# Attention visits placed 64 products earlier in a fused attention and feed-forward kernel

## The chip, the cores and the metric

The kernel runs on one core of a Trainium2 chip, as one program. The metric is the device time of one execution in microseconds; where several executions were timed, their median. The profile is of one execution.

## The reference

One transformer block on 2048 rows of width 1024, in bfloat16: windowed causal attention with 32 heads of 32, then a dense layer pair with SiLU, each behind a layer norm without gains, each added to its input.

```python
qkv = layernorm(x) @ wqkv                      # q, k, v of 32 heads, 32 wide
scores = q @ k.T * 32 ** -0.5                  # kept where 0 <= query - key < 256
h = x + (softmax(scores) @ v) @ wo
h2 = h + silu(layernorm(h) @ w1) @ w2          # w1: 1024 x 3584, w2: 3584 x 1024
```

## The kernel before

**Stages.** The 2048 rows are four blocks (0 to 3) of 512. The order of all work is written out by hand. After a start-up that normalises block 0 and makes its values (v), there are these stages, each made of groups of eight matmuls of 128x128 by 512 columns that accumulate in one PSUM bank. Such a matmul is called a *product* here.

1. Query and key groups of block 0: 16 groups, 128 products (`qk_group`, L262, copied out in L264 by ScalarE and VectorE in turn).
2. Block 1: 8 groups of v (`v_group`, L252 and L254) and 16 of queries and keys, 192 products.
3. Blocks 2 and 3, the same: 384 products.
4. The output projection of blocks 0 to 2 (`wo_group`, L283): 24 groups, 192 products. Its residual add on VectorE (L285) empties the bank, and each finished tile of 128 rows is stored to `h_dram` (L288) and later loaded again (L642) for the second layer norm.
5. The dense layers, block by block: 28 groups against w1 (`h1_group`, L746, with tanh in L755 and the product in L756), then w2 (L783, L798). The projection of block 3 lies among the w1 groups of block 0.

**Attention lies between the products.** The 32 heads are eight groups of four (G = 8) in each block; a group of heads is numbered i = 8 b + g. Before every product the function `between` of a stream object counts it and may issue one of two things:

- a *visit*: the score matmuls of some heads, the exps on ScalarE that read them, and the masks on GpSimd (`select`, L411). Block 0 has one visit per half of a head group (`scores_0`, matmuls L392, exps L401 to L403). Blocks 1 to 3 have three visits for a pair of head groups (`visit`, matmuls L360, exps L315, L321 and L322).
- a *piece*: the matmuls of two heads' probabilities with v (`attn_piece`, L421), into one PSUM bank `o_ps`, which VectorE then divides by the row sums (`attn_norm`, L432 and L433). Every second piece puts a DMA transpose (L441, on SP) on the list `late`, which is run ahead of the next group. It writes the result over the queries.

**Where they stand.** `First` counts from block 1's start: a visit of block 0 every 12 products, and from the fourth visit on a piece just ahead of it. `Stream` counts from block 2's start: pair p has its visits at products 4, 20 and 36 of 48 p, and its four pieces at 42, 47, 58 and 63. So a pair has 48 products; 12 pairs fill stages 3 and 4, block 0's last three pieces are done at the head of stage 3, and the last two pieces of all are left over (`rest`, `pending`) and issued behind the first two w1 groups.

**Shared buffers.** Scores have one tile `sc` of four PSUM banks, written by every visit; its next writer waits for ScalarE to have read it. There are four more banks. Three take the groups' sums in turn, each emptied by VectorE after its group; the fourth is `o_ps`. A visit also borrows these: `idle` is the bank of the next group, `behind` that of the group before, `out` is `o_ps`. Exp results lie in buffers (`xbuf`, `ybuf`, `c_ring`) of two or three copies.

**Layer norm steps.** The layer norm of the next block is cut into steps on VectorE (four of statistics, L193 and L201; four of the reciprocal root, L209 to L216; four that normalise, L221) and four DMA transposes on SP (L225). One follows most groups, from n = 1. In the projection, the second layer norm's steps for block 0 begin after group 11, the load of h after group 9, two steps a group from 14.

VectorE, ScalarE, GpSimd and SP each take their instructions in the order written.

Of the kernel before, what the change touches and what calls it, by code (L numbers as in the profile page):

```python
# [14 lines left out]
P = 128  # L15
# [32 lines left out]
def kernel(  # L48
# [280 lines left out]
    def visit(i, n):  # L329
# [4 lines left out]
        if n == 0:  # L334
            own, e_own = unit_xy(i, 0), xbuf(i)
            more = [(0, idle, unit_c(i)), (1, out, unit_c(i)), (2, behind, unit_c(i))]
        elif n == 1:
            own, e_own = unit_xy(i, 1), ybuf(i)
            more = [(3, idle, unit_c(i)), (0, behind, unit_xy(i + 1, 0)), (1, out, unit_xy(i + 1, 0))]
        else:  # L340
            own, e_own = unit_xy(i + 1, 1), ybuf(i + 1)
            more = [(2, out, unit_xy(i + 1, 0)), (3, behind, unit_xy(i + 1, 0))]
# [34 lines left out]
    def scores_0(g, odd):  # L377
# [20 lines left out]
        for pair in range(2):  # L398
            e = (ybuf if odd else xbuf)(g)[:, 1024 * pair:1024 * (pair + 1)].rearrange("p (h q) -> p h q", q=512)
            two = sc[:, pair * 2:pair * 2 + 2, :]  # L400
            nc.scalar.activation(out=e[:, :, 0:256], in_=two[:, :, 0:256], func=ACT.Exp, scale=scale)  # L401
            nc.scalar.activation(out=e[:, :, 320:512], in_=two[:, :, 256:448], func=ACT.Exp, scale=scale)
            nc.scalar.activation(out=c_ring[:, (g + 1) % 3, pair * 2:pair * 2 + 2, 128 + 64 * odd:192 + 64 * odd],  # L403
                                 in_=two[:, :, 448:512], func=ACT.Exp, scale=scale)
            select(e[:, :, 0:P], e[:, :, 0:P], True)
            select(e[:, :, 256:384], e[:, :, 320:448], False)
            select(e[:, :, 384:512], e[:, :, 384:512], True)
# [42 lines left out]
    class First:  # L450


        def __init__(self):
            self.pieces, self.done, self.seen = [], 0, 0

        def between(self, kt):
            if self.seen == self.done * 12:
                if self.done > 2:
                    attn_piece(*self.pieces.pop(0))
                scores_0(self.done // 2, self.done % 2)  # L460
                self.pieces.append((self.done // 2, self.done % 2))
                self.done += 1
            self.seen += 1

    class Stream:


        def __init__(self, left):
            self.seen = 0
            self.visits, self.pieces = {}, {0: left[0], 10: left[1], 15: left[2]}  # L470
            for p in range((NB - 1) * G // 2):
                i, t = G + 2 * p, 48 * p + 4
                for n in range(3):
                    self.visits[t + 16 * n] = (i, n)
                for n in range(4):
                    self.pieces[t + (38, 43, 54, 59)[n]] = (i + n // 2, n % 2)

        def between(self, kt):
            if self.seen in self.pieces:
                attn_piece(*self.pieces.pop(self.seen))  # L480
            if self.seen in self.visits:
                visit(*self.visits.pop(self.seen))
            self.seen += 1

        def rest(self):
            assert not self.visits
            return [self.pieces[at] for at in sorted(self.pieces)]

# [180 lines left out]
    stream = First()  # L669
# [12 lines left out]
    stream = Stream(stream.pieces)  # L682
    for b in range(2, NB):
# [12 lines left out]
        for n in range(24):  # L696
# [32 lines left out]
    pending = [lambda piece=piece: attn_piece(*piece) for piece in stream.rest()]  # L729
# [106 lines left out]
```

## Time and profile before

| | |
|---|---|
| median of 3 runs | 698.19 us (696.15 to 698.81) |
| the profiled execution | 696.58 us, of which the span from first to last instruction is 694.9 us |
| instructions | 14583 |
| granted TensorE clock | 1.00 throughout |
| HBM | 39.85 MB read, 8.39 MB written |

By stage, in microseconds from the span's start (edges read from the timeline):

| stage | from, to |
|---|---|
| start-up | 0, 20.6 |
| queries and keys of block 0 | 20.6, 48.2 |
| block 1, with block 0's attention | 48.2, 102.7 |
| blocks 2 and 3, with attention of blocks 1 and 2 | 102.7, 225.5 |
| projection of blocks 0 to 2, with attention of block 3 | 225.5, 290.1 |
| dense layers | 290.1, 694.9 |

How to read the rows: PE is TensorE's matmul, PEld its weight load, DVE is VectorE, ACT ScalarE, POOL GpSimd, SP the queue that issues DMAs. A timeline row gives the start, the length, engine, line, operation, tile written and tiles read, shapes, the count of instructions that are merged in it, and in brackets the engine's idle time before it and what ended that. The matmul's length includes a modelled pipeline; starts are what to compare. A group row ends with busy time, mean ns of one, and idle time before it. A row of waits gives total, times and longest.

### The profile page before, as it was taken

The numbers are of one execution on the slowest core, as the hardware profiler recorded it, in microseconds if no ns is written. First come the engines' busy times: TensorE is split into PE (matmuls) and PEld (weight loads), VectorE is DVE, ScalarE is ACT, GpSimd is POOL, SyncE is SP. The second block draws the span as 40 slices with busy tenths as digits, with TensorE's granted clock in tenths as the row PEclk, the third lists the DMA queues.
The fourth block names the chain that finished last, engine by engine and source line by source line (L and its number), as shares of the span: only waits on it lengthen the run. The fifth ranks groups of instructions, "written<-read, shape, count | busy, mean of one in ns | idle before, by whom it ended". The sixth has DMA issues, their size and how long they took to land.

```text
span 694.9 us, 14583 instructions
## 1 busy us (share of the span) xinstructions
PE 676.7 (97%) x6084; PEld 340.4 (49%) x6200; DVE 290.2 (42%) x614; ACT 241.9 (35%) x462; POOL 160.8 (23%) x295
## 2 busy tenths in 40 slices
PE   9999999999999997999999999999999999999998
PEld 4445555555555554544444444444444444444445
DVE  5268646744444457443316134434133251233111
ACT  7326666656666664521310023300033200233000
POOL 1016765576666655500000000000000000000000
PEclk9999999999999999999999999999999999999999
DMA  8741241027321895791123410023300024100010
GB/s 275 254 92 40 48 108 32 17 48 210 116 75 34 283 227 176 169 337 62 31 77 99 106 39 1 0 76 83 84 1 0 12 97 91 46 1 0 31 38 24
DMA packets 77617, 61.50 MB, mean 89 GB/s; under 512 B 52464, under 2 KB 60656, under 8 KB 77552
## 3 DMA queue, kind: packets, MB, share of 16 engines
q1 hardware_dynamic: 77408, 60.31, 31.5%
q8 instruction: 48, 0.79, 0.5%
q10 hardware_dynamic: 144, 0.26, 0.1%
q14 instruction: 17, 0.14, 0.1%
HBM read 39.85 MB, written 8.39 MB: 69 GB/s over the span
## 4 chain that ended last, share of the span: by engine, by line
PE 89%; ACT 5%; issue 2%; DVE 2%; DMA 1%; POOL 0%; ACTq 0%; DVEq 0%
PE hacc L783 16%; PE hacc L746 16%; PE bank L262 13%; PE bank L746 12%; PE bank L783 12%; PE bank L252 5%; PE bank L421 5%; PE bank L283 4%; ACT r_e L321 4%; PE sc L360 2%; PE bank L360 2%; ACT r_e L322 1%; PE bank L566 1%; PE hacc L283 1%; PE sc L392 1%
## 5 line engine op out<-in xcount | busy, mean ns | idle before, releaser
L411 POOL TENSOR_SCALAR_AFFINE_SELECT r_e<-r_e 128x512 bf16<-128x512 bf16 (+1 forms) x288 | 157.8, 564 | 130.3 <-ACT r_e L321 61.6
L783 PEld LDWEIGHTS <-r_a 128*128 128x128 bf16 x952 | 90.8, 98 | 103.0
L746 PEld LDWEIGHTS <-r_w 128*128 128x128 bf16 x896 | 87.4, 98 | 105.2
L783 PE MATMUL hacc<-r_a 128*128 128x512 bf16 (+2 forms) x550 | 114.0, 366 | 0.5
L746 PE MATMUL hacc<-r_e,r_w 128*128 128x512 bf16 x375 | 84.7, 379 | 0.5
L783 PE MATMUL bank<-r_a 128*128 128x512 bf16 (+1 forms) x386 | 81.0, 368 | 0.4
L755 ACT ACTIVATE r_n<-hacc 128x512 f32<-128x512 f32 x24 | 14.3, 597 | 172.2 <-PE hacc L746 122.7
L262 PEld LDWEIGHTS <-r_w 128*128 128x128 bf16 x512 | 46.5, 97 | 52.0 <-issue 1.0
L264 DVE CAST r_a<-bank 128x512 bf16<-128x512 f32 x56 | 38.6, 689 | 61.8 <-PE bank L262 48.3
L746 PE MATMUL bank<-r_e,r_w 128*128 128x512 bf16 x282 | 63.6, 379 | 0.3
L262 PE MATMUL bank<-r_t,r_w 128*128 128x512 bf16 x233 | 56.4, 379 | 2.3 <-issue 1.6
L262 PE MATMUL bank<-r_w 128*128 128x512 bf16 x240 | 55.9, 379 | 1.4 <-issue 0.8
L421 PEld LDWEIGHTS <-r_e 128*128 128x128 bf16 x1440 | 45.6, 96 | 18.6 <-issue 3.9
L321 ACT ACTIVATE r_e<-sc 128x1536 bf16<-128x1536 f32 x36 | 53.5, 1485 | 0.0
L283 PE MATMUL bank<-r_o,r_a 128*128 128x512 bf16 x201 | 49.8, 379 | 2.0 <-issue 1.1
L421 PE MATMUL bank<-r_a,r_e 128*128 128x33 bf16 x1440 | 46.2, 178 | 2.9 <-DVE r_n L433 2.9
L315 ACT ACTIVATE r_e<-bank 128x512 bf16<-128x512 f32 x48 | 26.1, 598 | 55.9 <-PE bank L360 53.6
L798 DVE SCALAR_TENSOR_TENSOR r_t<-bank,r_t 128x512 bf16<-128x512 f32 (+1 forms) x14 | 9.3, 663 | 67.5 <-PE bank L783 67.5
L798 DVE SCALAR_TENSOR_TENSOR r_t<-hacc,r_t 128x512 bf16<-128x512 f32 (+2 forms) x20 | 13.0, 650 | 52.6 <-PE hacc L783 52.6
L283 PEld LDWEIGHTS <-r_a 128*128 128x128 bf16 x256 | 22.9, 97 | 24.6
L360 PEld LDWEIGHTS <-r_a 32*64 32x64 bf16 x1536 | 21.2, 103 | 17.9 <-issue 16.5
L252 PE MATMUL bank<-r_w,r_t 128*128 128x512 bf16 x116 | 28.3, 379 | 1.2 <-issue 0.8
(103 smaller groups left out, 586.4 us busy)
## 6 DMA issues: line engine op xcount, KB each, us to landing
r_w<-in_B_w_dram SPq DMA_DIRECT2D x8, 896.0 KB, 5.3
r_a<-in_B_w_dram SPq DMA_DIRECT2D x7, 1024.0 KB, 9.0
r_w<-in_A_wqkv_dram SPq DMA_DIRECT2D x4, 1024.0 KB, 8.4
h_dram<-r_t SPq DMA_DIRECT2D x16, 256.0 KB, 2.4
r_t<-h_dram SPq DMA_DIRECT2D x16, 256.0 KB, 3.0
out_dram<-r_t SPq DMA_DIRECT2D x31, 128.0 KB, 1.7
r_e<-h_dram SPq DMA_DIRECT2D x3, 1024.0 KB, 5.8
r_o<-in_A_x_dram SPq DMA_DIRECT2D x11, 256.0 KB, 4.3
```

Source lines behind the costliest of these rows:

```text
L252: nc.tensor.matmul(acc, lhsT=lnT_b[b % 2][:, kt, j * P:(j + 1) * P], rhs=wv[:, kt, c * 512:(c + 1) * 512], start=(kt == 0), stop=(kt == KT ...
L262: nc.tensor.matmul(acc, lhsT=wqk[:, kt, col0:col0 + P], rhs=lnT_b[b % 2][:, kt, :], start=(kt == 0), stop=(kt == KT - 1))
L264: copy(out=(qT, kT)[which][b][:, g, :], in_=acc)
L283: nc.tensor.matmul(acc, lhsT=qT[b][:, g, j * P:(j + 1) * P], rhs=wo[:, g, c * 512:(c + 1) * 512], start=(g == 0), stop=(g == G - 1))
L315: nc.scalar.activation(out=c_ring[:, lo:hi + 1:hi - lo, h, :], in_=four[bank].rearrange("p (n q) -> p n q", q=256), func=ACT.Exp, scale=scale)
L321: nc.scalar.activation(out=tri_of(e)[:, h0:h1, :, 64:256], in_=tri, func=ACT.Exp, scale=scale)
L360: nc.tensor.matmul(bank[half * 64:half * 64 + 64, col:col + qb - qa], lhsT=kT[t // 4][r0:r0 + DH, g, k0:k0 + 64], rhs=qT[b][r0:r0 + DH, g, ...
L411: nc.gpsimd.affine_select(out=dst, in_=src, pattern=[[0, n] for n in dst.shape[1:-1]] + [[sgn, P]], compare_op=ALU.is_ge if upper else ALU ...
L421: nc.tensor.matmul(o_ps[:, qt * 2 + hh, 0:VW], lhsT=chunk_of(i, bank, piece, pair * 2 + hh), rhs=v[:, b * 4 + kt, g * 4 + pair * 2 + hh, : ...
L746: nc.tensor.matmul(acc, lhsT=w1[:, kt, ft * P:(ft + 1) * P], rhs=ln2T[b][:, kt, :], start=(kt == 0), stop=(kt == KT - 1))
L783: nc.tensor.matmul(acc[:, 0:c1 - c0], lhsT=gT[:, ft, j * P:(j + 1) * P], rhs=w2[ft // 4][:, ft % 4, c0:c1], start=(ft == 0), stop=(ft == F ...
L798: nc.vector.scalar_tensor_tensor(out=t_out[j % 2][:, c0:c1], in0=acc[:, 0:c1 - c0], scalar=0.5, in1=t_in[j % 2][:, c0:c1], op0=ALU.mult, o ...
```

## The change

One class `Attention` takes the place of `First` and `Stream`. It counts from the first product of stage 1.

- Block 0's 16 visits stand every 10 products from product 92, so the first four fall in stage 1. Its pieces stand every 10 products from 122, the last two at 267 and 284.
- Pair p starts at 256 + 48 p instead of, in the same count, 320 + 48 p. Its visits stay at 4, 20 and 36; its pieces are at 41, 46, 59 and 76. The last piece is at 860, and stage 4 ends with product 895; nothing is left over for the dense layers.
- In block 0's visits, three exps over four heads replace six over two heads, and three masks replace six.
- In the second visit of a pair, heads 0 and 1 of the side scores trade the banks `out` and `behind`, so the exp of `out` comes ahead.
- The copies of block 0's groups 11 to 15 are all VectorE's. `run_late` is called ahead of each group of stage 1.
- In blocks 2 and 3, layer-norm steps follow odd groups only, one while more than eight are left and then two; transposes follow even groups, when no step is left.

```diff
         elif n == 1:
             own, e_own = unit_xy(i, 1), ybuf(i)
-            more = [(3, idle, unit_c(i)), (0, behind, unit_xy(i + 1, 0)), (1, out, unit_xy(i + 1, 0))]
+            more = [(3, idle, unit_c(i)), (0, out, unit_xy(i + 1, 0)), (1, behind, unit_xy(i + 1, 0))]
...
-        for pair in range(2):
-            e = (ybuf if odd else xbuf)(g)[:, 1024 * pair:1024 * (pair + 1)].rearrange("p (h q) -> p h q", q=512)
-            two = sc[:, pair * 2:pair * 2 + 2, :]
-            nc.scalar.activation(out=e[:, :, 0:256], in_=two[:, :, 0:256], func=ACT.Exp, scale=scale)
-            nc.scalar.activation(out=e[:, :, 320:512], in_=two[:, :, 256:448], func=ACT.Exp, scale=scale)
-            nc.scalar.activation(out=c_ring[:, (g + 1) % 3, pair * 2:pair * 2 + 2, 128 + 64 * odd:192 + 64 * odd],
-                                 in_=two[:, :, 448:512], func=ACT.Exp, scale=scale)
-            select(e[:, :, 0:P], e[:, :, 0:P], True)
-            select(e[:, :, 256:384], e[:, :, 320:448], False)
-            select(e[:, :, 384:512], e[:, :, 384:512], True)
+        e = (ybuf if odd else xbuf)(g)[:, 0:2048].rearrange("p (h q) -> p h q", q=512)
+        nc.scalar.activation(out=e[:, :, 0:256], in_=sc[:, :, 0:256], func=ACT.Exp, scale=scale)
+        nc.scalar.activation(out=e[:, :, 320:512], in_=sc[:, :, 256:448], func=ACT.Exp, scale=scale)
+        nc.scalar.activation(out=c_ring[:, (g + 1) % 3, :, 128 + 64 * odd:192 + 64 * odd], in_=sc[:, :, 448:512],
+                             func=ACT.Exp, scale=scale)
+        select(e[:, :, 0:P], e[:, :, 0:P], True)
+        select(e[:, :, 256:384], e[:, :, 320:448], False)
+        select(e[:, :, 384:512], e[:, :, 384:512], True)
...
-    class First:
...
-    class Stream:
...
+    class Attention:
         def __init__(self):
             self.seen = 0
+            self.visits, self.pieces = {}, {}
+            for d in range(2 * G):
+                self.visits[92 + 10 * d] = lambda d=d: scores_0(d // 2, d % 2)
+                self.pieces[(122 + 10 * d, 267, 284)[max(d - 13, 0)]] = (d // 2, d % 2)
             for p in range((NB - 1) * G // 2):
-                i, t = G + 2 * p, 48 * p + 4
+                i, t = G + 2 * p, 256 + 48 * p
                 for n in range(3):
-                    self.visits[t + 16 * n] = (i, n)
+                    self.visits[t + 4 + 16 * n] = lambda i=i, n=n: visit(i, n)
                 for n in range(4):
-                    self.pieces[t + (38, 43, 54, 59)[n]] = (i + n // 2, n % 2)
+                    self.pieces[t + (41, 46, 59, 76)[n]] = (i + n // 2, n % 2)
...
+    stream = Attention()
     steps = sum(ln1_steps(1), [])
     for g0 in range(0, G, 4):
         for w in range(2):
             for g in range(g0, g0 + 4):
-                qk_group(0, w, g, dve if g % 2 else act)
+                run_late()
                 n = g0 * 2 + w * 4 + g % 4
+                qk_group(0, w, g, dve if g % 2 or n > 10 else act, stream.between)
...
             dense[n]()
-            if steps and n >= 1 and n != 3:
-                steps.pop(0)()
-            elif turns and n % 3 == 2:
+            if n % 2:
+                for _ in range(1 if len(steps) > 8 else 2):
+                    if steps:
+                        steps.pop(0)()
+            elif turns and not steps:
                 turns.pop(0)()
...
-    pending = [lambda piece=piece: attn_piece(*piece) for piece in stream.rest()]
+    assert not stream.visits and not stream.pieces
...
-        extra = []
-        if b == 0:
-            extra = [(f, 1) for f in pending]
-            pending = []
...
-            if extra:
-                extra.pop(0)[0]()
```

More of the change, by code (lines that the diff above doesn't have):

```diff
@@ L481, in between @@
             if self.seen in self.visits:
-                visit(*self.visits.pop(self.seen))
+                self.visits.pop(self.seen)()
             self.seen += 1
-        def rest(self):
-            assert not self.visits
-            return [self.pieces[at] for at in sorted(self.pieces)]
     dve, act = nc.vector.tensor_copy, nc.scalar.copy
@@ L668 @@
     steps, turns = ln1_steps(2)
-    stream = First()
     dense = [lambda j=j, c=c: v_group(1, j, c, dve, stream.between) for j in range(4) for c in range(2)]
@@ L679 @@
     assert not steps and not turns
-    stream = Stream(stream.pieces)
     for b in range(2, NB):
```

11 lines of the change are left out of this document (removed).

## The prediction

> **What bounds the kernel now.** I read the page, then the PE busy time by stage, then the short list of what PE waits for, and last the timeline of single stretches.
>
> ```profile
> PE 676.7 (97%) x6084; PEld 340.4 (49%) x6200; DVE 290.2 (42%) x614; ACT 241.9 (35%) x462; POOL 160.8 (23%) x295
> ```
> ```profile
> 48.20:105.00 56.80, 55.13 (x802) 30.50 (x818) 34.66 (x81) 35.16 (x97) 37.75 (x96) 1.00 0.34 79
> 105.00:225.50 120.50, 115.32 (x2073) 67.65 (x2112) 61.05 (x138) 79.82 (x144) 78.13 (x126) 1.00 0.29 76
> 225.50:290.10 64.60, 59.20 (x1068) 34.56 (x1088) 36.38 (x85) 39.95 (x72) 40.34 (x65) 1.00 0.83 219
> ```
> ```profile
> PE bank L421 <- DVE r_n L433: 2.9, 3, 1.5
> PE bank L360 <- DVE r_t L285: 1.0, 1, 1.0
> ```
>
> The columns of the stretches are length, then PE, PEld, DVE, ACT, POOL busy, granted clock, DMA share, GB/s. The clock is 1.00, and TensorE is idle for only 1.7, 5.2 and 5.4 us in the three stages that hold attention (block 1; blocks 2 and 3; the output projection). TensorE bounds the kernel everywhere. The change takes no work from TensorE, so it can win only its stalls, and those are small. I price them one by one.
>
> A **steady pair** of head groups (timeline, dense work of block 2):
>
> ```profile
> 140.63 0.43 PE L360 MATMUL sc<-r_a 32*64 32x320 bf16 x24
> 144.35 0.66 ACT L322 ACTIVATE r_e<-sc 128x512 bf16<-128x512 f32 x1
> 145.06 0.43 PE L360 MATMUL sc<-r_a 32*64 32x320 bf16 x24
> 146.95 0.76 PE L421 MATMUL bank<-r_a,r_e 128*128 128x33 bf16 x24
> 148.63 0.76 PE L421 MATMUL bank<-r_a,r_e 128*128 128x33 bf16 x24
> 155.85 0.43 PE L360 MATMUL sc<-r_a 32*64 32x320 bf16 x24
> ```
>
> One pair lasts 155.85 - 140.63 = 15.22 us. Between its second visit (140.63) and its third (145.06) lie 16 products, 3.45 us (a product is 0.216 us, below), and the second visit's own scores, about 0.7, with 0.09 to change over: 4.25, yet 4.43 pass. The third visit writes the score tile `sc`, which ACT releases at 144.35 + 0.66 = 145.01, just ahead of 145.06. So TensorE **waits 0.18 us for ACT** in each of the 12 pairs: 2.1 us. Two output pieces five products apart start 1.68 us apart: 1.08 of products and 0.60 of piece.
>
> **Stalls behind a layer-norm step.** At the start of block 2, and in the output projection:
>
> ```profile
> 115.57 0.76 PE L421 MATMUL bank<-r_a,r_e 128*128 128x33 bf16 x24
> 116.02 1.28 DVE L193 BATCH_NORM_STATS2 ln_st<-r_o 128x6 f32<-128x512 bf16 x2
> 117.65 0.42 DVE L433 TENSOR_TENSOR r_n<-bank,recip 128x256 bf16<-128x256 f32 x1
> 118.13 0.76 PE L421 MATMUL bank<-r_a,r_e 128*128 128x33 bf16 x24 [0.70 <-DVE r_n L433]
> ```
> ```profile
> 256.88 0.43 PE L360 MATMUL sc<-r_a 32*64 32x320 bf16 x24
> 257.94 1.29 DVE L193 BATCH_NORM_STATS2 ln_st<-r_a 128x6 f32<-128x512 bf16 x2 [0.78 <-DMA r_a<-h_dram]
> 262.16 0.77 PE L421 MATMUL bank<-r_a,r_e 128*128 128x33 bf16 x24 [1.45 <-DVE r_n L433]
> 269.89 0.41 PE L360 MATMUL bank<-r_a 32*64 32x320 bf16 x10 [0.99 <-DVE r_t L285]
> 274.09 0.75 PE L421 MATMUL bank<-r_a,r_e 128*128 128x33 bf16 x24 [0.71 <-DVE r_n L433]
> 275.86 0.43 PE L360 MATMUL sc<-r_a 32*64 32x320 bf16 x24
> ```
>
> The pieces of 115.57 and 118.13 are 2.56 us apart instead of 1.68: 0.9 us lost, since the first one's normalisation (L433) stands in DVE's queue behind a statistics step (L193), and the second piece needs its bank. In the projection the pair from 256.88 to 275.86 takes 18.98 instead of 15.22: **3.8 us** lost, in three such waits. Stalls of attention in all: 2.1 + 0.9 + 3.8 = 6.8 us. That is the most that this change can win.
>
> **The change part by part.** *Block 0's visits every 10 products, from product 92 of its query/key stage.*
>
> ```profile
> 60.75 0.61 PE L421 MATMUL bank<-r_a,r_e 128*128 128x33 bf16 x18
> 61.29 0.42 PE L392 MATMUL sc<-r_a 32*64 32x320 bf16 x16
> 61.65 2.76 PE L252 MATMUL bank<-r_w,r_t 128*128 128x512 bf16 x11
> 61.85 0.60 ACT L401 ACTIVATE r_e<-sc 128x512 bf16<-128x512 f32 x1 [1.30 <-PE sc L392]
> 62.34 0.49 ACT L402 ACTIVATE r_e<-sc 128x384 bf16<-128x384 f32 x1
> 62.71 0.28 ACT L403 ACTIVATE r_e<-sc 128x128 bf16<-128x128 f32 x1
> 64.25 0.61 PE L421 MATMUL bank<-r_a,r_e 128*128 128x33 bf16 x18
> ```
>
> Twelve products take 64.25 - 61.65 = 2.60 us, so one takes 0.216. Piece and scores cost TensorE 61.65 - 60.75 = 0.90 a visit, and that stays: 16 score visits and 16 pieces are moved, none removed. The period falls from 3.50 to 2.16 + 0.90 = 3.06 us; while there is no piece yet (two gaps) it is about 2.6. What it has to cover is the turn-around of `sc`. The six exps become three over twice as many elements, the six selects three.
>
> ```profile
> L505 ACT ACTIVATE r_e<-r_o 128x1024 bf16<-128x1024 bf16 x2 | 2.1, 1057 | 0.3 <-DMA r_o<-in_A_x_dram 0.3
> L411 POOL TENSOR_SCALAR_AFFINE_SELECT r_e<-r_e 128x512 bf16<-128x512 bf16 x192 | 120.1, 640 | 68.2 <-ACT r_e L321 61.6
> L411 POOL TENSOR_SCALAR_AFFINE_SELECT r_e<-r_e 128x256 bf16<-128x256 bf16 x96 | 37.8, 413 | 62.1 <-ACT r_e L401 60.0
> ```
>
> POOL falls from 6 x 0.41 to 3 x 0.64 = 1.9 us a visit. The 1024-element exp takes about 1.06 (nearest row, another function), but the next one starts some 0.1 us before an exp ends (61.85 + 0.60 against 62.34), so I take 0.95, 0.7 and 0.4: 2.05. `sc` is free 0.56 (61.29 to 61.85) + 2.05 = 2.6 us after a visit starts: under 3.06, level with 2.6. Bounds: 1.7 by elements alone (0.60 - 0.28 = 0.32 for 384 more, 2048 of them), and 2 x (0.60 + 0.49 + 0.28) = 2.74 if the merging saves nothing and no exp overlaps another: `sc` back after 3.3, 0.24 lost 13 times and 0.7 twice, 4.5 in all. I take **0**, by the 1.06 of the nearest row. The selects lie under the 30 products until the piece.
>
> The Trainium skill, "ScalarE: Activation LUTs", section "Rules for kernel authors", gives about 0.3 us per ACTIVATE and 0.83 ns per element. By that the three exps would take 2.6 us and `sc` would come back after 3.2 us, over the period: about 0.1 x 13 + 0.6 x 2 = 2.5 us lost, a sum of -1.2. The trace does not agree: the same figures give the present six exps 3.5 us, and the period of 3.50 has no gap.
>
> *DVE in block 1.* Its steps stay at every group. With a period of 3.06 a normalisation behind a copy (0.7) and a statistics step (1.5) ends about 3.1 us after the group starts. At product 152, the first of its group after two consecutive statistics steps, the next piece is due about 0.3 earlier: **+0.3**.
>
> *Pairs 64 products ahead, pieces at 41, 46, 59 and 76.* Piece 76 now stands 8 products behind the next pair's second visit, between it and the third, so 0.60 us more of TensorE's work covers ACT's release of `sc`: the 0.18 goes, **-2.1**. What is late next is the bank shared by scores and outputs: at 8 products, 1.73 us, its exp must be done; with the swapped order it is second on ACT, about 1.3 us after the scores (0.2 until the first exp, 0.5 for 512 elements, 0.6 for 384 + 128, as the starts in block 0 are apart). Third, without the swap, would be about 1.9 and would stall. The pieces at 41 and 46 come one product sooner after the third visit, whose exp of that bank is first: covered by 0.4 us.
>
> *Layer-norm steps after odd groups.* Visits at 4, 20 and 36 fall in even groups, pieces in odd ones. A step then follows the copy into a group that has no piece, and is over (0.3 + 0.7 + 1.5 = 2.5) when that group's 1.73 + 0.7 is: **-0.9**. If block 2's last transposes were later than block 3 asks for, this would show, but the last is issued one group sooner than now.
>
> *The projection.* Its layer-norm steps are not changed, only what they meet. The visits and pieces fall elsewhere: pieces at 121 and 126, both in group 15 of the stage. After group 14 DVE does the residual add, statistics and the first step of the root.
>
> ```profile
> 248.16 0.52 SPq L288 DMA_DIRECT2D h_dram<-r_t  x1
> 252.15 0.38 SPq L642 DMA_DIRECT2D r_a<-h_dram  x1
> 267.93 0.60 DVE L209 TENSOR_SCALAR ln_var<-st_b 128x4 f32<-128x4 f32 x1
> 283.98 1.23 SPq L225 DMA_TRANSPOSE r_a<-r_a  x1
> 290.12 1.89 PE L746 MATMUL bank<-r_a,r_w 128*128 128x512 bf16 x8
> ```
> ```profile
> 40.09 0.17 DVE L209 TENSOR_SCALAR ln_var<-st_a 128x4 f32<-128x4 f32 x1
> ```
> ```profile
> r_a<-r_a SPq DMA_TRANSPOSE x4, 4.5
> ```
>
> The piece's normalisation ends 0.3 + 0.6 + 1.5 + 0.6 to 1.2 + 0.6 = 3.6 to 4.2 us after group 14; TensorE is ready for piece 126 after 1 product, a piece and 5 products, 1.9 us. It waits 1.7 to 2.3: I take 2.0. Ahead of that, visit 116 needs the bank of group 13, whose add stands behind a normalisation and a statistics step: 0.3. The store and load of h (248.16, 252.15, statistics at 257.94) end as close to group 11 as now. Later pieces (139, 156) each have a free group before them. So **3.8 becomes 2.3**; bounds 0.6 and 4.
>
> "SBUF — State Buffer" of the Trainium skill, section "Who interferes with whom", says that a VectorE operation in a two-port mode, or with two SBUF inputs, is shut out while GpSimd reads SBUF. The trace agrees (0.60 beside selects, 0.17 without), and without that rule piece 126 would wait 1.7.
>
> *The stage border.* All attention now ends at product 156 of 192, so no piece is left for the first dense group, and the same piece time moves ahead of it: no gain. But the 36 last products have no cover. The last transpose of the layer norm is issued at 283.98, lands 4.5 later at 288.5, and is needed at 290.12: 1.6 us to spare, 9.8 us after group 19 ends. Now only 4 groups, 6.9 us, follow group 19. If the transpose keeps its 3.6 + 4.5 = 8.1, TensorE waits 1.2; if SP, which has less queued ahead of it, issues it 2.5 after group 19, it waits 0.1. I take **+0.5**.
>
> Sum: -2.1 - 0.9 - 1.5 + 0.3 + 0.5 = **-3.7 us**. The profiled execution took 696.58 us (span 694.9), so its like would take 692.9. The median of the runs is 698.19, 1.6 above it, so I forecast 694.5.
>
> **Rivals.** (a) *Every stall goes*: projection and border cost nothing. For: DVE is 56% busy there. Then -6.5, 691.7. (b) *It does little of what it says*: the projection's stalls stay at 3.8 or the wait for `sc` is replaced by a wait for the output bank of piece 76. For: the margins that I found for that bank and for the pieces at 41 and 46 are only 0.4 us. -1, 697.2. (c) *ACT sets block 0's pace*: the upper bound of the exps holds, -3.7 + 4.5 = +0.8, 699.0. For: `sc` has one copy, and two gaps are level with my own 2.6. Against: in the present period exps do overlap, and twelve products run at 2.60 without a gap. The Trainium skill's figures ("ScalarE: Activation LUTs") point the same way, as said. (d) *Slower*: the chain load of h, statistics, root, four transposes becomes the bound at the border, as its cover shrinks by 2.9 us. Each us by which the last transpose lands later than 6.9 after group 19 is a us of idle TensorE. From 4.2 the gain is gone; by 0.5% slower it takes 7.7, and I put it at 8: 702. For: the load already makes DVE wait 0.78. Against: 4.5 us is a median of four.
>
> **How the numbers follow.** Forecast 0.51, (a) 0.16, (b) 0.17, (c) 0.05, (d) 0.11. The bound of 0.5%, about what a measurement can tell, is 3.5 us, so the forecast's own range, -2.3 to -5.2 (693 to 696), lies on both sides, some six tenths below. Faster 0.32 + 0.16 = 0.48; within 0.19 + 0.17 + 0.05 = 0.41; slower 0.11. The range goes from (a) to (b), each with an allowance of 1 us for the scatter of the runs, and leaves (c) and (d) out with 0.16: 690.8 to 698.2.
>
> **What would show it.** Right: pair periods of 15.04 and no wait between second and third visit; no PE wait on L433 in blocks 2 and 3; one of about 2 us at the second piece of group 15; the first product of the dense layer within 1 us of the last projection product; block 0's visits 3.06 apart. Wrong: score matmuls of block 0 waiting for ACT, a gap of several us at the border, or pairs longer than 15.2.

## The result, and the profile after

The changed kernel takes 692.52 us in the median of 4 runs (691.73 to 693.31); the kernel before took 697.67 beside it (696.15 to 698.81, 4 runs). The ratio is 0.9928, with an interval of 0.9903 to 0.9952: **faster by 0.7%**. The forecast was 694.5, in a range from 690.8 to 698.2. The profiled execution took 692.04 us with a span of 690.3, against 696.58 and 694.9: 4.5 us less, where the sum said 3.7.

The engines' row of the page after, then the busy time by stage (block 1; blocks 2 and 3; the output projection; columns as in the prediction), then what PE waits for, with total, times and longest in us (a wait at the start of the program is left out):

```profile
PE 684.0 (99%) x6200; PEld 338.5 (49%) x6200; DVE 295.4 (43%) x616; ACT 237.7 (34%) x412; POOL 155.5 (23%) x247
```
```profile
48.20:88.60 40.40, 40.40 (x631) 22.73 (x630) 30.45 (x72) 26.33 (x41) 25.82 (x41) 1.00 0.38 72
88.60:218.00 129.40, 129.40 (x2357) 73.00 (x2356) 68.11 (x150) 86.00 (x156) 85.40 (x136) 1.00 0.35 85
218.00:286.70 68.70, 66.27 (x1032) 36.21 (x1029) 38.88 (x90) 34.00 (x62) 36.82 (x59) 1.00 0.74 212
```
```profile
PE bank L419 <- DVE r_n L431: 1.9, 1, 1.9
...
PE bank L360 <- DVE r_t L285: 0.3, 1, 0.3
PE bank L360 <- DVE r_n L431: 0.2, 1, 0.2
```

In the first two stages PE busy equals the length of the stretch, so the page shows no gap there. (The length of a matmul is modelled, and a wait of 0.1 us hides in it, see block 0's visits below.) All other waits for DVE stand in the projection, in three places. (The trace of before misses some matmul records, 6084 of 6200, so a part of its gaps was no idle time; lengths are therefore compared from start to start, below.)

A steady pair after, from the timeline of all engines; it begins with the second visit, and the pieces are now L419:

```profile
124.53 0.69 DVE L254 CAST r_a<-bank 128x512 bf16<-128x512 f32 x1 [0.35 <-PE bank L252]
125.28 0.43 PE L360 MATMUL sc<-r_a 32*64 32x320 bf16 x24
125.53 0.41 PE L360 MATMUL bank<-r_a 32*64 32x320 bf16 x20
125.87 1.90 PE L252 MATMUL bank<-r_w 128*128 128x512 bf16 x8
127.61 0.77 PE L419 MATMUL bank<-r_a,r_e 128*128 128x33 bf16 x24
128.90 0.65 ACT L322 ACTIVATE r_e<-sc 128x512 bf16<-128x512 f32 x1
130.04 0.43 PE L360 MATMUL sc<-r_a 32*64 32x320 bf16 x24
```
```profile
140.19 0.32 PE L360 MATMUL sc<-r_a 32*64 32x320 bf16 x2
```

The pair lasts 140.19 - 125.28 = 14.91 us; before it was 15.22. ACT releases `sc` at 128.90 + 0.65 = 129.55, and the third visit comes at 130.04: that wait is gone, by 0.5 us. The visit's own matmuls last 125.87 - 125.28 = 0.59 us. Before they lasted 0.70 (140.63 to 141.33, when the dense products went on), and DVE's and PE's timelines of before show why:

```profile
140.24 0.68 DVE L264 CAST r_a<-bank 128x512 bf16<-128x512 f32 x1
```
```profile
140.97 0.42 PE L360 MATMUL bank<-r_a 32*64 32x320 bf16 x20
```

The scores that go into the bank of the last dense group started 0.34 us after the visit (140.63), just behind the copy that empties this bank (140.24 + 0.68 = 140.92), and the copy was late because the normalisation (L433) of the last piece, four products ahead of the visit, stood before it in DVE's queue until 140.32. After, the copy ends at 125.22, ahead of the visit, and those scores follow 0.25 us after it. That is a second wait of the old pair, of 0.1 us, and the prediction did not see it.

Block 0's visits and their exps, timeline of after:

```profile
46.14 0.42 PE L392 MATMUL sc<-r_a 32*64 32x320 bf16 x16
46.64 1.02 ACT L399 ACTIVATE r_e<-sc 128x1024 bf16<-128x1024 f32 x1 [0.56 <-PE sc L392]
47.56 0.80 ACT L400 ACTIVATE r_e<-sc 128x768 bf16<-128x768 f32 x1
48.25 0.39 ACT L401 ACTIVATE r_e<-sc 128x256 bf16<-128x256 f32 x1
49.20 0.43 PE L392 MATMUL sc<-r_a 32*64 32x320 bf16 x24
```

They are 49.20 - 46.14 = 3.06 us apart, as forecast, and `sc` is back 48.64 - 46.14 = 2.50 us after a visit starts (forecast 2.6). One gap is longer, between these two rows of PE's timeline:

```profile
58.41 0.42 PE L392 MATMUL sc<-r_a 32*64 32x320 bf16 x16
61.57 0.43 PE L392 MATMUL sc<-r_a 32*64 32x320 bf16 x24
```

They are 3.16 us apart. Two statistics steps (56.95 and 58.94) stand in DVE's queue ahead of the normalisation of the piece before, which ends at 60.99, and the next piece starts at 61.04 instead of 60.94: 0.1 us lost, at the place that the prediction named (product 152).

What is left in the projection, by PE's timeline and then DVE's:

```profile
264.20 0.43 PE L360 MATMUL sc<-r_a 32*64 32x320 bf16 x24
264.87 0.32 PE L360 MATMUL bank<-r_a 32*64 32x320 bf16 x2 [0.24 <-DVE r_n L431]
265.46 0.41 PE L360 MATMUL bank<-r_a 32*64 32x320 bf16 x10 [0.27 <-DVE r_t L285]
265.80 1.25 PE L283 MATMUL bank<-r_o,r_a 128*128 128x512 bf16 x5
267.50 1.24 PE L283 MATMUL bank<-r_o,r_a 128*128 128x512 bf16 x5
270.65 0.75 PE L419 MATMUL bank<-r_a,r_e 128*128 128x33 bf16 x24 [1.92 <-DVE r_n L431]
```
```profile
262.15 0.69 DVE L285 TENSOR_TENSOR r_t<-bank,r_a 128x512 bf16<-128x512 f32 x1 [1.05 <-DMA h_dram<-r_t]
270.18 0.42 DVE L431 TENSOR_TENSOR r_n<-bank,recip 128x256 bf16<-128x256 f32 x1
```

Visits and pieces are numbered here by the product of the stage, as in the prediction. Visit 116 takes 265.80 - 264.20 = 1.60 us instead of 0.58: 1.0 lost. Piece 126 starts 270.65 - 267.50 = 3.15 us after five products that need 1.08: 2.1 lost, behind the statistics step and the root's first step, which hold up the normalisation until 270.60.

The border, from PE's timeline:

```profile
278.94 7.93 PE L283 MATMUL bank<-r_o,r_a 128*128 128x512 bf16 x36
286.76 3.61 PE L729 MATMUL bank<-r_a,r_w 128*128 128x512 bf16 x16
```

The 36 last products begin at 278.94, 36 x 0.216 = 7.8 later the dense layer goes on without a gap. The trace has the last transpose issued at 283.18 and landing at 286.67, 0.1 us ahead of that.

### The profile page after: what moved, and what is told of

Read it like the earlier page. It is cut to its first block, busy times and chain, and to the rows that moved or that the text cites. A ratio compares the mean times of both kernels' runs of the same rounds, so it can differ in the third digit from the quotient of the medians.

```text
span 690.3 us, 14586 instructions
## 1 busy us (share of the span) xinstructions
PE 684.0 (99%) x6200; PEld 338.5 (49%) x6200; DVE 295.4 (43%) x616; ACT 237.7 (34%) x412; POOL 155.5 (23%) x247
## 4 chain that ended last, share of the span: by engine, by line
PE 97%; DVE 1%; DMA 1%; issue 0%; DVEq 0%
PE bank L262 17%; PE hacc L760 16%; PE hacc L729 16%; PE bank L729 12%; PE bank L760 12%; PE bank L252 7%; PE bank L283 6%; PE bank L419 5%; PE sc L360 2%; PE bank L360 1%; PE bank L547 1%; PE hacc L283 1%; DMA h_dram<-r_t 1%; PE sc L392 1%; PE tp L252 1%; PE bank L186 0%
## 5 line engine op out<-in xcount | busy, mean ns | idle before, releaser
L409 POOL TENSOR_SCALAR_AFFINE_SELECT r_e<-r_e 128x512 bf16<-128x512 bf16 x240 | 152.5, 643 | 115.2 <-ACT r_e L399 52.8
L264 DVE CAST r_a<-bank 128x512 bf16<-128x512 f32 x58 | 40.0, 689 | 52.9 <-PE bank L262 33.7
L262 PE MATMUL bank<-r_t,r_w 128*128 128x512 bf16 x256 | 61.3, 379 | 0.0
L262 PE MATMUL bank<-r_w 128*128 128x512 bf16 x256 | 59.4, 379 | 0.0
L419 PEld LDWEIGHTS <-r_e 128*128 128x128 bf16 x1440 | 45.6, 96 | 17.4 <-issue 2.6
L283 PE MATMUL bank<-r_o,r_a 128*128 128x512 bf16 x224 | 52.6, 379 | 0.0
L419 PE MATMUL bank<-r_a,r_e 128*128 128x33 bf16 x1440 | 46.2, 178 | 1.9 <-DVE r_n L431 1.9
L252 PE MATMUL bank<-r_w,r_t 128*128 128x512 bf16 x128 | 30.5, 380 | 0.0
L321 ACT ACTIVATE r_e<-bank 128x384 bf16<-128x384 f32 x48 | 23.8, 495 | 16.8 <-PE bank L360 14.5
```

Source lines behind the costliest of these rows:

```text
L252: nc.tensor.matmul(acc, lhsT=lnT_b[b % 2][:, kt, j * P:(j + 1) * P], rhs=wv[:, kt, c * 512:(c + 1) * 512], start=(kt == 0), stop=(kt == KT ...
L262: nc.tensor.matmul(acc, lhsT=wqk[:, kt, col0:col0 + P], rhs=lnT_b[b % 2][:, kt, :], start=(kt == 0), stop=(kt == KT - 1))
L264: copy(out=(qT, kT)[which][b][:, g, :], in_=acc)
L283: nc.tensor.matmul(acc, lhsT=qT[b][:, g, j * P:(j + 1) * P], rhs=wo[:, g, c * 512:(c + 1) * 512], start=(g == 0), stop=(g == G - 1))
L321: nc.scalar.activation(out=tri_of(e)[:, h0:h1, :, 64:256], in_=tri, func=ACT.Exp, scale=scale)
L409: nc.gpsimd.affine_select(out=dst, in_=src, pattern=[[0, n] for n in dst.shape[1:-1]] + [[sgn, P]], compare_op=ALU.is_ge if upper else ALU ...
```

## The experiments

**Theory A**: the gain is the sum of the priced waits (the new places of the pieces with the swapped order of the shared scores, the odd layer-norm steps, a part of the projection's stalls), and that attention runs 64 products ahead is worth nothing by itself. **Theory B**, the rival: it is the earlier attention that pays, since it takes the last pieces out of the dense layer and gives everything more room. Later runs test the prediction's rivals (c), ACT in block 0, and (d), the border, and then what the projection still holds.

**x1_pieces_swap**: the kernel before with the swap and the new piece distances, at the old place.

```diff
-            more = [(3, idle, unit_c(i)), (0, behind, unit_xy(i + 1, 0)), (1, out, unit_xy(i + 1, 0))]
+            more = [(3, idle, unit_c(i)), (0, out, unit_xy(i + 1, 0)), (1, behind, unit_xy(i + 1, 0))]
...
-                    self.pieces[t + (38, 43, 54, 59)[n]] = (i + n // 2, n % 2)
+                    self.pieces[t + (37, 42, 55, 72)[n]] = (i + n // 2, n % 2)
```

> The kernel before, with two edits of the change only: a pair's pieces at 41, 46, 59 and 76 of its 48 products (in the old count), and the second visit's exp of the output bank ahead. Attention stays at its old place. Theory A (the gain is the priced waits; the shift by itself is worth nothing): the pair's period falls from 15.22 to about 14.9 us, 12 pairs, so 3.5 to 3.9 us less than before, a ratio of about 0.995; the waits behind layer-norm steps (0.9 and 3.8 us before) stay, give or take 1.5 us, as their places are moved against the pieces. Theory B (attention placed earlier is what pays): no change beyond 1 us, period 15.2.

Measured: 692.63 (692.27 to 694.17, 4 runs) against 696.59 of the kernel before on this chip, ratio 0.9948 (0.9933 to 0.9963). In blocks 2 and 3 a pair is 14.90 to 14.91 us from the third on (first visits at 134.85 and 149.76 in PE's timeline), as in the changed kernel. Two lines of the change, without any shift, give 4.0 us.

**x2_shift_only**: the changed kernel with the swap undone, the pieces at their old distances and the old layer-norm steps.

```diff
-            more = [(3, idle, unit_c(i)), (0, out, unit_xy(i + 1, 0)), (1, behind, unit_xy(i + 1, 0))]
+            more = [(3, idle, unit_c(i)), (0, behind, unit_xy(i + 1, 0)), (1, out, unit_xy(i + 1, 0))]
...
-                self.pieces[(122 + 10 * d, 267, 284)[max(d - 13, 0)]] = (d // 2, d % 2)
+                self.pieces[(122 + 10 * d, 266, 271)[max(d - 13, 0)]] = (d // 2, d % 2)
...
-                    self.pieces[t + (41, 46, 59, 76)[n]] = (i + n // 2, n % 2)
+                    self.pieces[t + (42, 47, 58, 63)[n]] = (i + n // 2, n % 2)
...
-            if n % 2:
-                for _ in range(1 if len(steps) > 8 else 2):
-                    if steps:
-                        steps.pop(0)()
-            elif turns and not steps:
+            if steps and n >= 1 and n != 3:
+                steps.pop(0)()
+            elif turns and n % 3 == 2:
```

> The changed kernel with only the shift kept (block 0's visits every 10 products from product 92 with merged exps, all pairs 64 products ahead): pieces at 42, 47, 58, 63, the exps' order and the layer-norm steps as in the kernel before. Theory A: pairs of 15.2 us again, waits behind layer-norm steps of 3 to 5 us, so within 1.5 us of the kernel before, ratio 0.998 to 1.002. Theory B: most of the gain stays, 3.5 to 5 us faster than before.

Measured: 698.74 (698.25 to 699.77, 6 runs) against 696.59, ratio 1.0033 (1.0020 to 1.0046): a little slower than before, and worse than theory A's narrow band; against theory B in sign. From its list of PE waits:

```profile
PE bank L419 <- DVE r_n L431: 4.5, 5, 1.7
...
PE bank L360 <- issue: 0.7, 1, 0.7
PE bank L727 <- issue: 0.6, 1, 0.6
```

The shift sets each piece against other layer-norm steps. Before there were three waits on the normalisation and one on the residual add, 2.9 + 1.0 = 3.9 us; with the old distances at the new place there are five, one at a visit of the projection, and an idle time at the border (L727): 4.5 + 0.7 + 0.6 = 5.8. That is 1.9 more, of the 2.1 that the medians differ by. The steady pairs are 15.2 us, as in before.

**x3_no_swap** and **x4_old_pieces**: the changed kernel with one of the two lines undone.

```diff
x3_no_swap
-            more = [(3, idle, unit_c(i)), (0, out, unit_xy(i + 1, 0)), (1, behind, unit_xy(i + 1, 0))]
+            more = [(3, idle, unit_c(i)), (0, behind, unit_xy(i + 1, 0)), (1, out, unit_xy(i + 1, 0))]
x4_old_pieces
-                    self.pieces[t + (41, 46, 59, 76)[n]] = (i + n // 2, n % 2)
+                    self.pieces[t + (42, 47, 58, 63)[n]] = (i + n // 2, n % 2)
```

> The changed kernel with the swap of the second visit's banks undone. Theory A: the output bank's exp is third on ACT and ends about 2.5 us after the visit starts, the piece eight products later is due at 2.33 and waits 0.15; and the scores that go to the bank of the group before wait about 0.1 for its copy again: pairs of 15.1 to 15.2 instead of 14.9, a span 2 to 3.5 us longer than the changed kernel's 690.3. Theory B: no difference beyond 0.5 us.

> The changed kernel with the pieces back at 42, 47, 58 and 63, all else kept. Theory A: the time from second to third visit is then set by ACT alone (4.43 us in the kernel before), so the pair is 15.2 us again although the swap stays: the wait of the third visit for ACT grows from 0.18 to about 0.28 as the second visit's own scores got 0.1 shorter. 12 pairs: 3.5 us longer than 690.3, plus or minus 1.5 for the projection's waits. If the swap's 0.1 were a gain by itself: pairs of 15.1, 2.2 us longer. Theory B: no difference beyond 1 us.

Measured: 693.66 and 695.04, one run each. The pairs are 15.03 to 15.07 and 15.17 to 15.21. ACT's and PE's timelines of x3_no_swap at the second visit (125.09) and the piece 8 products behind it:

```profile
127.21 0.31 ACT L322 ACTIVATE r_e<-bank 128x128 bf16<-128x128 f32 x1
```
```profile
127.57 0.77 PE L419 MATMUL bank<-r_a,r_e 128*128 128x33 bf16 x24
```

Without the swap the bank's exp comes third and ends at 127.52; the piece starts at 127.57, 2.48 us after the visit instead of 2.33 (125.28 to 127.61 above). So the swap is worth 0.15 us a pair with the new piece, as the prediction's sentence on the bank had it, and nothing without: with the swap and the old distances (x4_old_pieces) the pair is 15.2 as before. PE's and ACT's timelines there:

```profile
141.00 0.43 PE L360 MATMUL sc<-r_a 32*64 32x320 bf16 x24
145.41 0.43 PE L360 MATMUL sc<-r_a 32*64 32x320 bf16 x24
```
```profile
144.70 0.66 ACT L322 ACTIVATE r_e<-sc 128x512 bf16<-128x512 f32 x1
```

The third visit again comes right behind ACT's release (144.70 + 0.66 = 145.36). The moved pieces alone take 15.22 to 15.05, both lines take it to 14.91.

**x5_old_steps**: the changed kernel with the old layer-norm steps in blocks 2 and 3 (the last hunk of x2_shift_only alone).

> The changed kernel with block 3's layer-norm steps again after nearly every group of block 2. Theory A: a statistics step then stands in DVE's queue ahead of the piece at 41, and the piece at 46 waits about 1.1 us for its bank; perhaps 0.2 more once; nothing else moves: 1.0 to 1.4 us longer than 690.3, start-up aside. Rival: the pieces' new places alone cleared that wait, and the steps' order is worth nothing: within 0.3 us.

Measured: 694.45, one run. PE's timeline:

```profile
119.22 0.75 PE L419 MATMUL bank<-r_a,r_e 128*128 128x33 bf16 x24 [1.28 <-DVE r_n L431]
```

Two pairs become 16.35 and 15.54 instead of 14.95 and 14.91, so the odd steps are worth 2.0 us at the new place, more than expected because a second pair waits too (0.41 at the piece of 134.76).

**x6_six_exps**: the changed kernel with the old six exps and six selects a visit in block 0 (that hunk of the change undone).

> The changed kernel with block 0's visits of six exps and six masks again, still every 10 products. Theory A: six exps overlap at their starts, the score tile comes back 2.7 us after a visit starts, below the period of 3.06 us: no wait in the visits with a piece, up to 0.1 in the two without, within 0.5 us of 690.3. Rival (exps cost their full length one behind the other, 0.56 + 2.74 = 3.3): 0.24 in 13 visits and 0.7 in two, 4.5 us longer. By the Trainium skill, ScalarE: Activation LUTs, 0.3 us an ACTIVATE and 0.83 ns an element, the tile would come back after 4.06 us, and the loss would be about 13 to 16 us.

Measured: 693.88, one run. ACT's and PE's timelines at the visit of 46.00:

```profile
48.37 0.33 ACT L403 ACTIVATE r_e<-sc 128x128 bf16<-128x128 f32 x1
```
```profile
46.00 0.42 PE L392 MATMUL sc<-r_a 32*64 32x320 bf16 x16
```

Six exps give `sc` back 48.70 - 46.00 = 2.70 us after the visit starts, three give it back after 2.50, and the visits with a piece stay 3.06 apart. The two gaps without a piece grow from 2.61 and 2.63 us to 2.75 and 2.81, so all visits of block 0 together took 0.3 us more. Rival (c) falls: merging the exps was not needed for the period of 3.06, and is worth 0.3 us. The 4.06 us that the expectation works out from the Trainium skill ("ScalarE: Activation LUTs", section "Rules for kernel authors") are not borne out; the page gives its 0.3 us for an ACTIVATE whose bias is a pointer operand, and these exps are given no bias. The rest of what this run is longer lies in the projection (the clock, in the last section).

**x8_ln2_late**: the changed kernel with the second layer norm's steps starting after group 14 instead of 11, so that the last transpose is issued later.

```diff
-            if steps and n >= 11:
+            if steps and n >= 14:
```

> The changed kernel with the second layer norm's steps for block 0 begun after group 14 instead of 11, two a group, so that the last transpose is issued one group later. It measures what is left at the stage border. Theory A (no slack left there: the last transpose lands just as the first dense product is due): a gap of 1.5 to 2.5 us ahead of that product; the wait of visit 116 goes, that of piece 126 grows to about 2.5 to 3. Rival (a slack of 2 us or more is left): no gap at the border.

Measured: 697.04, one run. PE's timeline at the border:

```profile
290.13 5.27 PE L729 MATMUL bank<-r_a,r_w 128*128 128x512 bf16 x16 [2.72 <-issue]
```

The trace has the last transpose landing at 289.93, and TensorE stands still for 2.7 us at the border, a little longer than expected. The wait of visit 116 is gone and that of piece 126 is 2.3. So the chain of rival (d) is real, it was only 0.1 us short of deciding in the changed kernel. Sixteen products then take 5.1 us (290.13 to 295.24) instead of 3.45, the clock again.

**x7_ln2_early** and **x9_ln2_apart**: can the projection's 3.1 us be won? Both load h tile by tile and spread the statistics steps; they differ in where these stand.

```diff
-        steps = [load]
+        loads = [lambda j=j: nc.sync.dma_start(out=hb[:, j, :], in_=h_dram[(b * 4 + j) * P:(b * 4 + j + 1) * P, :]) for j in range(4)]
+        steps = [load] if b else loads
...
x7_ln2_early: the tile loads after groups 3, 5, 7, 9
+        for _ in range({5: 1, 7: 1, 9: 1, 11: 1, 13: 2, 15: 2, 16: 1}.get(n, 2 if n > 16 else 0)):
x9_ln2_apart: the tile loads after groups 5, 7, 9, 11
+        for _ in range({7: 1, 9: 1, 11: 1, 13: 1, 15: 4, 16: 2, 17: 2, 18: 2, 19: 2}.get(n, 0)):
```

> The changed kernel with the second layer norm's steps for block 0 spread out in the projection: h is loaded tile by tile after groups 3, 5, 7 and 9, statistics follow groups 5, 7, 9 and 11, the root groups 13 and 15, so that no statistics step stands ahead of a piece; the last steps stay where they were. Theory A: the waits of visit 116 and of piece 126, 1.0 and 2.1 us, go, and nothing takes their place: 3 us shorter than 690.3, a ratio to the kernel before of about 0.989. Rival (the chain of the layer norm, or SP's queue behind four more waiting loads, becomes the bound at the border): the 3 us come back as a gap ahead of the first dense product, within 0.5 us of the changed kernel.

> The changed kernel with the second layer norm's steps for block 0 kept apart from pieces, and its tile loads kept out of SP's way: loads of h after groups 5, 7, 9 and 11, each some three groups behind its store, statistics after groups 7, 9, 11 and 13, the root after 15, then two steps a group to 19. Theory: the waits of visit 116 (1.0) and piece 126 (1.9 to 2.1) go, no store and no residual add waits for SP, the last transpose is issued a group earlier: span about 687.2 with the start-up of 690.3, and as no idle time is long enough to lower the granted clock, every run at clock 1.000: median 1 us lower still against the changed kernel's runs, 3.5 to 4.5 us in all. Rival: SP's order or the transposes' landing takes the place of those waits, as it did when the loads were issued after groups 3 to 9: within 1 us of the changed kernel.

Measured: x7_ln2_early 692.95 (692.19 to 695.19, 6 runs), ratio 0.9933 (0.9915 to 0.9951), no better than the changed kernel. x9_ln2_apart 689.06 (688.45 to 689.96, 6 runs) against 696.97, ratio 0.9876 (0.9854 to 0.9897). The timeline of all engines in x7_ln2_early:

```profile
247.72 0.33 SPq L624 DMA_DIRECT2D r_a<-h_dram  x1
249.21 0.38 SPq L288 DMA_DIRECT2D h_dram<-r_t  x1
255.46 0.69 DVE L285 TENSOR_TENSOR r_t<-bank,r_a 128x512 bf16<-128x512 f32 x1 [3.48 <-DMA h_dram<-r_t]
256.77 0.75 PE L419 MATMUL bank<-r_a,r_e 128*128 128x33 bf16 x24 [3.76 <-DVE r_n L431]
```

A tile load is queued on SP before the store of its tile has landed (issued at 240.94, landed at 247.70 by the trace), and the load stands there until then, 247.72. The store of the next tile is queued behind it: its last residual add ended at 243.71, yet it goes out at 249.21 and lands at 255.27. The residual add that needs its buffer again waits 3.5 us for this landing, the normalisation behind the add waits, and the piece waits 3.8. In x9_ln2_apart the loads come two groups later, and such a wait is not seen. The projection stage of x9_ln2_apart by busy time, from the same start to its first dense product:

```profile
218.00:284.40 66.40, 66.40 (x1057) 36.81 (x1055) 38.07 (x90) 34.84 (x62) 37.62 (x60) 1.00 0.80 213
```

The page shows no gap of TensorE in it, and its list of waits has none for attention. This version beats both kernels: by 4.1 us the changed one, which took 693.12 on the same chip (the next run).

**x10_changed_again**: the changed kernel once more, on the chip of x9_ln2_apart.

> The changed kernel itself, again, beside the others on one chip. If the wait at piece 126 sometimes lowers the granted clock for a window of 3.4 us and sometimes does not, its executions fall into two groups, at clock 1.000 and 0.998, about 1.3 to 1.7 us apart (first seen: 692.04 and 691.73 against 693.0 and 693.31). If the spread has another cause, time and clock do not go together.

Measured: 693.12 (691.62 to 694.15, 6 runs), ratio 0.9935 (0.9914 to 0.9957), the first result again. Time and clock go together, as expected (last section).

**x11_no_shift** and **x12_no_shift_apart**: the kernel before with most of the change but the shift: x1_pieces_swap, the odd steps of the change in blocks 2 and 3, and tile loads of h after groups 5, 7, 9 and 11 as in x9_ln2_apart. Block 0's visits keep their six exps and the period of 12 products. The two differ in the second layer norm's steps.

```diff
x11_no_shift
+        for _ in range({7: 1, 9: 1, 11: 1, 13: 1, 15: 4, 17: 3, 19: 4, 20: 1}.get(n, 0)):
x12_no_shift_apart
+        for _ in range({7: 1, 9: 1, 11: 1, 13: 1, 14: 1, 15: 2, 17: 3, 18: 2, 19: 3, 20: 1}.get(n, 0)):
```

> All of the change but the shift, and the second layer norm's steps kept apart, on the kernel before: attention at its old place, block 0's visits every 12 products with six exps, two pieces left over into the dense layers; pieces at 41, 46, 59 and 76, the swapped banks, steps after odd groups; tile loads and steps of the projection after odd groups only. Theory A (the shift itself is worth nothing): as fast as the changed kernel with its projection mended, within 1 us. Theory B (the shift is worth something once the other waits are gone): 2 us slower or more.

> The kernel of x11 with the root's four steps no longer in one go after group 15 (there they stood ahead of two pieces, a wait of 2.5 us, and lowered the clock for a window): one after 14, two after 15, one after 17, the rest to 20. Theory A (the shift is worth nothing once the other waits are gone): no wait on attention left, every run at clock 1.000, as fast as x9, which has the shift: 688.5 to 690, ratio 0.986 to 0.990. Theory B (the shift is worth something): 691 or more, with the difference to x9 in pairs longer than 14.91 or in a gap at the border to the dense layers.

Measured: x11_no_shift 693.68 (693.36 to 694.09, 6 runs), ratio 0.9943 (0.9923 to 0.9963). That is 4.6 us above x9_ln2_apart, which the expectation would have put down to theory B. But its own steps make a new wait (its list of PE waits):

```profile
PE bank L421 <- DVE r_n L433: 2.5, 1, 2.5
```

Four steps after group 15 stand ahead of two pieces, the pair there takes 18.96 us instead of 14.91, and so the run decides nothing by itself. With those steps spread, x12_no_shift_apart takes 689.16 (688.84 to 689.30, 6 runs) against 697.52, ratio 0.9873 (0.9849 to 0.9897), and attention waits for DVE nowhere. That is the ratio of x9_ln2_apart (0.9876), which has the shift; in the profiles the two take 666.7 and 666.4 us from the first query/key product to the end. **Once no piece and no visit waits behind a layer-norm step, these runs show no difference between attention at its old place and 64 products earlier.** Theory A is shown and theory B falls.

## Why the prediction was right

The mechanism was right: TensorE bounds the kernel, the change can only win its stalls, and most of those that were priced are won. The sizes were off in both directions, and that the sum came out within 2 us is in part luck: the pairs gave 1.6 us more than forecast, the projection 0.8 less. Term by term, forecast first:

- **Pairs: -2.1, measured 12 x (14.91 - 15.22) = -3.7.** The step that mis-sized it is the reading of the second visit: "the second visit's own scores, about 0.7" was taken as work, while 0.1 of it was a wait for the copy of a dense bank, made late by the last piece's normalisation. The same four pieces, moved, remove both waits. It makes 0.28 of the 0.31, with the 0.18 of `sc`. (x4_old_pieces has the swap with the old pieces, and its visit still takes 0.69.) The other claim of that step, that the swapped order is needed for piece 76, is shown by x3_no_swap (0.15 a pair).
- **Layer-norm step at block 2's start: -0.9, measured -0.9.** No wait for L431 in that stage, and x5_old_steps brings waits back.
- **Projection: 3.8 to 2.3, measured 3.8 to 3.1.** Piece 126 waits 2.1, forecast 2.0. The term that was wrong is visit 116: 0.3 forecast, 1.0 measured. The forecast had the store and the load of h "as close to group 11 as now"; the residual add ahead of the visit waited 1.05 for an earlier store to land (the DVE row at 262.15), which the trace has issued at 255.41 and landed at 262.03, beside the load of h. The 0.3 counted DVE's queue and left out the DMAs that it waits for. Which one is late differs: in x10_changed_again, the same kernel, the first statistics step waits for the load of h, and visit 116 loses 1.9 us, so that the projection's stalls are 4.0 there:

```profile
261.16 1.29 DVE L193 BATCH_NORM_STATS2 ln_st<-r_a 128x6 f32<-128x512 bf16 x2 [2.14 <-DMA r_a<-h_dram]
```

It takes the statistics steps as well: in x8_ln2_late, where none stands there, the add waits 2.69 us for its store and the visit does not wait.
- **Block 1: +0.3, measured +0.1**, the gap of 3.16 us above.
- **Border: +0.5, measured 0**, with 0.1 us to spare. The last transpose is issued 3.3 us after group 19 and lands 3.5 later, 6.8 of the 6.9. The forecast took 4.5 for the landing, the median of four; the last one, which alone counts, had landed after 3.3 us before too (283.98 to 287.26), so 2.9 us were to spare there and not 1.6.

- **Block 0's visits: 0, measured 0.** The six exps would have cost 0.3 us (x6_six_exps).

The sum of the measured terms is -3.7 - 0.9 - 0.7 + 0.1 = -5.2. The trace has, for the part from the first query/key product to the first product against w2, before and after (PE's timelines):

```profile
20.46 1.89 PE L262 MATMUL bank<-r_w 128*128 128x512 bf16 x7
353.49 1.24 PE L783 MATMUL bank<-r_a 128*128 128x512 bf16 x5
```
```profile
20.95 1.24 PE L262 MATMUL bank<-r_w 128*128 128x512 bf16 x5
348.92 1.46 PE L760 MATMUL bank<-r_a 128*128 128x512 bf16 x6
```

333.03 and 327.97: -5.1. The start-up took 0.5 us longer in the profiled execution after; between executions of these kernels it ends anywhere between 20.2 and 21.8 us, so nothing shows it to be the change. What comes after is equal. -5.1 + 0.5 = -4.6, the difference of the spans.

The rivals: (a), every stall goes, is not what this change does, but x9_ln2_apart shows that it can be had, with 689.06. From the first query/key product to the end it is 8.0 us shorter than the kernel before, so the 6.8 that the prediction called the most were too few, by the pairs' second wait. (b) had it right that the projection's stalls hardly shrink (3.1, and 4.0 in x10_changed_again, instead of 3.8), but the bank of piece 76 made no wait and the pairs gave the gain. (c) fell. (d) did not come about, but its mechanism is shown by x8_ln2_late; with 0.1 us of cover left, it was near.

## What to carry to other kernels

When the bounding engine is 97% busy by its page, look for the gain in the places where its instructions meet another engine's queue, and compare the length of the same short piece of work in two places: a visit that takes 0.70 us here and 0.59 there holds a wait that no list of waits names. Moving a whole stage earlier paid nothing here, as the same meetings happen there; it only dealt them out anew, which x2_shift_only paid with 0.3%. And a load that depends on a store belongs so far behind it in the queue that it never has to wait there.

## What the runs showed of the hardware

**A short idle of TensorE can cost almost as much again in clock.** In x10_changed_again the same 1.92 us wait at piece 126 as above was followed by this (PE's timeline, then the stretches by busy time with the granted clock behind POOL):

```profile
271.16 0.75 PE L419 MATMUL bank<-r_a,r_e 128*128 128x33 bf16 x24 [1.92 <-DVE r_n L431]
```
```profile
265.00:272.40 7.40, 4.83 (x73) 2.85 (x73) 6.23 (x16) 3.04 (x6) 4.35 (x7) 1.00 0.44 123
272.40:275.80 3.40, 3.40 (x9) 1.21 (x8) 1.81 (x9) 0.00 (x0) 0.00 (x0) 0.50 0.34 86
```

For 3.4 us the granted clock is 0.50, so 1.7 us are lost on top of the 1.9. Of five profiled waits of 1.9 to 2.0 us at that piece it followed two (here and in x6_six_exps) and not the others (the profile after, x3_no_swap, x5_old_steps); it followed each of the four waits of 2.3 to 3.8 us (x7_ln2_early, x8_ln2_late twice, x11_no_shift) and none of those of up to 1.7 us in attention (before, x2_shift_only, x4_old_pieces). In both cases that were followed, the wait lies whole within the 3.41 us just ahead of the half clock (here 269.24 to 271.16 of 268.99 to 272.40). Where it lay in the three others their traces do not tell, so that this decides is not shown. It goes with a part of the scatter: the six runs of x10_changed_again had a mean clock of 1.000 at 691.62 and of 0.997 to 0.998 at 692.88 to 694.15, while all runs of x9_ln2_apart and x12_no_shift_apart, whose profiles have no such wait, had 1.000. The kernel before had 0.995 to 0.998 in 9 of the 42 runs that were taken beside the experiments; no trace of these nine is kept. The Trainium skill, "TensorE: Matmul & The Clock Gate", section "What's actually happening", puts the activity window at 4096 cycles of 1.2 GHz, 3413 ns, running freely; the length of the stretch at half clock agrees with that. Its section "Why this matters for your kernels" warns of idle gaps of more than about 3 us; here 1.9 us were enough in two profiles of five.

**Exps in a row overlap.** The three exps of block 0 start 0.92 and 0.69 us apart though they last 1.02 and 0.80 (46.64, 47.56, 48.25). Merging six instructions into three saved 0.2 us of 2.7.

**SP's queue keeps its order.** In x7_ln2_early a load that waits for a store until 247.72 holds up the store behind it, to 249.21, and the residual add that needs this store's buffer waits 3.5 us.
